# w3 and w_out chunks converted as one piece, ScalarE two units and VectorE one unit ahead, room for eight chunks, first loads on one queue

## The chip, the core and the metric

The kernel runs on one core of a Trainium2 chip. The core has five engines, each with an instruction queue that it works through in order: TensorE (PE in the profile; PEld is its weight load), VectorE (DVE), ScalarE (ACT), GpSimd (POOL) and SyncE (SP, which here only issues DMAs; ACT can issue DMAs too). They meet through semaphores. Matrix products go to PSUM, eight banks of 128 x 512 fp32, and are read from there by DVE or ACT.

The metric is the device time of one execution in microseconds. Three runs of the kernel before took 868.15, 868.35 and 868.7 us; the median is 868.35 us.

## The reference

```python
kv = np.einsum('bhsd,bhse->bhde', k, v)             # B, H, S, D = 8, 8, 576, 64
out = np.einsum('bhsd,bhde->bhse', q, kv)
rms = np.sqrt(np.mean(out * out, axis=-1, keepdims=True) + 1e-06)
x = (out / rms * g_norm)                            # then (B, H, S, D) -> (4608, 512)
a = x @ w1                                          # 512 x 1024
b = x @ w2
h = a * b @ w3                                      # 1024 x 1024
y = h @ w_out                                       # 1024 x 512
```

The weights arrive as 64-bit floats: `setup_inputs` scales fp32 arrays by a numpy scalar of 64 bits, which makes them double. Their conversion to fp32 is part of the kernel.

## The kernel before

**Stages.** The kernel first multiplies w3 by w_out once (the *fold*), so that each group of 512 tokens needs only x @ w1, x @ w2, the elementwise product, and one product with w3 @ w_out. Then it goes through nine groups: eight of 512 tokens, one for each batch, and a ninth made of the 64 tokens that each batch has left over. The products of a group are done by Winograd's scheme with seven products in place of eight (`winograd`, L436), on sums and differences of operand blocks that DVE prepares (`sum_w`, `combine_x` and the like).

**Conversion.** A 64-bit number lies in memory as two 32-bit words. `convert` (L127) makes fp32 of them with six instructions: ACT turns the low word into a small float (`low`, L135) and takes the absolute value of the high word read as fp32 (L136); DVE clamps that (L137), shifts its bits by three (L140), puts the sign bit into `low` (L143) and adds the two bit patterns (L147, a custom instruction, in the profile CUSTOM_DVE_ANT_0, in the lists of instructions ISA). The weights come in 20 *units* of 128 x 1024 numbers (1 MB as 64-bit floats), in the order of `todo` (L156): eight "c" units, each with the columns of the first half of w3 for one chunk and the chunk's 128 rows of w_out; four "b" units, each with the second half of w3 for two chunks; eight "w" units of w1 and w2. I number them 0 to 19: 0 to 7 are c, 8, 9, 11 and 13 are b, the rest w. Four raw buffers (`RAW = 4`) hold loaded units. `convert_next` (L194) converts the next unit and then has the load issued that takes its raw buffer (`load_next`, L164). A c unit is converted in two pieces of 512 columns, its w3 part and its w_out part (unit 0 in three); b and w units in one piece of 1024.

**The fold.** Two halves of eight chunks each. For a chunk, PE transposes four 128 x 128 blocks of w3 (`turn_w3`, L409, into a PSUM bank named `at`), ACT copies them to w3T (L416), and PE multiplies them with the chunk of w_out (`fold_chunk`, L420), adding over the chunks into four PSUM banks named `mm`. After the last chunk of a half, DVE and ACT copy two banks each to `w3o_sb` (L433, L431). The profile shows a step as eight matmuls of 128 x 512 (two for each product in the code) and four transposes. There are five `mm` banks and three `at` banks, and `w3_sb` holds two converted w3 pieces.

Half 0 has, for each chunk c: transposes of chunk c + 1, conversion of the unit after that, products of chunk c. Half 1 also carries the attention of the first batch, for four pairs of heads: `begin` (products of k and v, transposes of q, the loads of later heads), `middle` (product of q with kv, then the norm: square on ACT, sum on DVE, root on ACT, reciprocal and scaling on DVE) and `turn` (transposes of the result, copied with a scale to `xT` by ACT). After the fold, `sum_w(0)` and `combine_x(0)` prepare the operands of the first group on DVE, and the groups' loop begins; what is left of the conversion (units 16 to 19) stands in the first group.

**What sets the order.** PE's instructions are in the order of the code throughout. Those of DVE, ACT and SP are in the order of the code within the fold (`manual_schedule`, L613), and elsewhere a scheduler places them, which may also move instructions of later code into gaps that it sees in the fold.

**Names.** The lists of instructions and the profile leave out buffer numbers, and with them the digit of `w3_sb`: in the fold, `w_sb` is mostly the tile `w3_sb`; in conversions of w units it is the real `w_sb`.

Of the kernel before, what the change touches and what calls it, by code (L numbers as in the profile page):

```python
# [19 lines left out]
def kernel(  # L20
# [85 lines left out]
    def load_q_left(b):  # L106
# [5 lines left out]
        )  # L112


    w_sb = const.tile([P, KF, 2, NP, P], FP32, name="w_sb")
# [10 lines left out]

    def convert(dst, raw):  # L127
        if raw.dtype == FP32:
            nc.vector.tensor_copy(out=dst, in_=raw)
            return  # L130
        words = raw.bitcast(U32).rearrange("p (n w) -> p n w", w=2)
        lo, hi = words[:, :, 0], words[:, :, 1]
        low = conv_pool.tile([P, 1024], FP32, name="low", bufs=2)[:, 0:raw.shape[1]]
        dst_bits, low_bits = dst.bitcast(U32), low.bitcast(U32)
        nc.scalar.activation(low, lo, AF.Copy, scale=2.0 ** -51, bias=2.0)  # L135
        nc.scalar.activation(dst, hi.bitcast(FP32), AF.Abs)  # L136
        nc.vector.tensor_scalar(  # L137
            out=dst, in0=dst, scalar1=LEAST, scalar2=MOST, op0=ALU.max, op1=ALU.min
        )
# [3 lines left out]
        nc.vector.scalar_tensor_tensor(  # L143
            out=low_bits, in0=hi, scalar=0x80000000, in1=low_bits,
            op0=ALU.bitwise_and, op1=ALU.bitwise_or,
        )
        nc.vector.tensor_tensor(out=dst_bits, in0=dst_bits, in1=low_bits, op=ALU.add)  # L147
# [4 lines left out]

    NF = KF // 2
    RAW = 4
# [8 lines left out]

    def load_next(queue=nc.sync):  # L164
        if len(raws) == len(todo):
# [3 lines left out]

        def load(where, src, engine=nc.sync):  # L170
            engine.dma_start(out=raw[:, where].rearrange("p (c m) -> p c m", c=src.shape[1]), in_=src)

# [16 lines left out]
        raws.append(raw)  # L189

    converted = []
    w3_sb = {}

    def convert_next():  # L194
        n = len(converted)
        what, i = todo[n]
        if what == "w":
            convert(w_sb[:, i].rearrange("p w c f -> p (w c f)"), raws[n])
        elif what == "b":
            w3_sb["b", i] = fold.tile([P, 1024], FP32, name="w3_sb", bufs=2)  # L200
            convert(w3_sb["b", i], raws[n])
        else:
            t = w3_sb["c", i] = fold.tile([P, 1024], FP32, name="w3_sb", bufs=2)[:, 0:512]
            for cols in [slice(0, 512)] if i else [slice(0, 256), slice(256, 512)]:
                convert(t[:, cols], raws[n][:, cols])
            convert(wo_sb[:, i, :], raws[n][:, 512:1024])
        converted.append(n)
        load_next()
# [26 lines left out]
    def attention(b):  # L235
# [140 lines left out]
        if b == 0:  # L376
            return begin, middle, turn
        pieces = [
# [23 lines left out]

    ab = [const.tile([P, 4, N], FP32, name=f"ab{p}") for p in range(NF)]


    NH = KF // 2
    w3T = {}

    def turn_w3(half, c):  # L409
        t = w3_sb["b", c // 2] if half else w3_sb["c", c]  # L410
        t = t.rearrange("p (m f) -> p m f", m=NH)[:, :, (c % 2) * P * half:][:, :, 0:P]
        t_ps = bank(ps_at, "at").rearrange("p (m f) -> p m f", m=NH)
        for m in range(NH):
            nc.tensor.transpose(t_ps[:, m, :], t[:, m, :], ident)  # L414
        w3T[half, c] = fold.tile([P, NH, P], FP32, name="w3T", bufs=3)
        nc.scalar.copy(w3T[half, c], t_ps)  # L416

    sums_ps = {}

    def fold_chunk(half, c):  # L420
        if c == 0:
            sums_ps[half] = [bank(ps_mm, "mm") for m in range(NH)]
        for m in range(NH):
            nc.tensor.matmul(  # L424
                sums_ps[half][m], lhsT=w3T[half, c][:, m, :], rhs=wo_sb[:, c, :],
                start=(c == 0), stop=(c == KF - 1),
# [78 lines left out]
    xb, wa, aa, ob = {}, {}, {}, {}  # L505
    free = {}
    o_sbs = []

    def allocate():

        h = NP // 2
        for p in reversed(range(NF)):
            free["w", p] = late_pool.tile([P, 3, 2, h, P], FP32, name=f"ws{p}")
# [19 lines left out]
    def combine_x(T):  # L533
        xb[T] = {f"b{i + 1}{j + 1}": xT[T][:, i, j] for i in range(2) for j in range(2)}
        t = late_pool.tile([P, 3, NP // 2, N], FP32, name="xc")
        return combine(xb[T], parts(t))

# [41 lines left out]
    def project(T, between=lambda: None):  # L579
# [31 lines left out]
    fold = fold_cm.__enter__()  # L611
    wo_sb = fold.tile([P, KF, DM], FP32, name="wo_sb")
    in_order = tc.manual_schedule(  # L613
        engines={mybir.EngineType.DVE, mybir.EngineType.Activation, mybir.EngineType.SP}
    )
    with in_order:
        for _ in range(RAW):
            load_next(nc.scalar)
        g_src = g_norm.rearrange("(d o) -> d o", o=1)
        for e in range(2):  # L620
            nc.scalar.dma_start(out=g_col[e * D:(e + 1) * D, :], in_=g_src)
        nc.scalar.activation(const.tile([P, 1], FP32, name="warm"), eps_col, AF.Sqrt)


        keep_warm(14)
        convert_next()
        turn_w3(0, 0)
        convert_next()
        for c in range(KF):
            if c + 1 < KF:  # L630
                turn_w3(0, c + 1)
            else:
                turn_w3(1, 0)
            convert_next()
# [9 lines left out]
        begin, middle, turn = attention(0)  # L644
        AT = {1: 0, 3: 1, 4: 2, 5: 3}
        for c in range(KF):
            if c + 1 < KF:
                turn_w3(1, c + 1)
            if c in AT:
                begin(AT[c])  # L650
            if c < 6:
                convert_next()
            fold_chunk(1, c)
            if c in AT:
                middle(AT[c])
            if c - 1 in AT:
                turn(AT[c - 1])
    fold_cm.__exit__(None, None, None)
    late_pool = ctx.enter_context(tc.tile_pool(name="late", bufs=1, reuse_waits="tile"))
    allocate()  # L660
    run(sum_w(0), combine_x(0))

    for T in range(NG):
# [5 lines left out]
        for p in range(NF):  # L669
            gates(T, p, between if T or p else lambda: None)  # L670
            if T == 0:
                if p + 1 < NF:
                    run(sum_w(p + 1))
                for _ in range(2):
                    if len(converted) < len(todo):
                        convert_next()
                if p + 1 == NF:
# [39 lines left out]
```

## Time and profile before

| | |
|---|---|
| median of three runs | 868.35 us |
| the profiled execution | 869.37 us |
| its span, first to last instruction | 867.6 us |
| PE busy in the span | 830.0 us (96%) |
| DVE busy | 386.8 us (45%) |
| ACT busy | 267.5 us (31%) |
| granted PE clock, mean | 0.985 |
| DMA | 59.45 MB, mean 69 GB/s |

The shares are means over stages that differ. The page's row of 40 slices shows that DVE and ACT are busy mostly in the first six slices (130 us), that DMA moves 205 to 270 GB/s in the first five and little later, and that the granted clock falls below 0.9 only in the first, third and fifth slices. So the profile is read by stages: a table of windows first, then who waited for whom in the first stages, then single instructions in order of time. A row of such a list has the start in us, the length, engine and line, operation, output and input with their sizes, the number of instructions merged into the row, and in brackets how long the engine had been idle and what ended that.

### The profile page before, as it was taken

How to read it: one execution, taken by the hardware profiler on the slowest of the kernel's cores; microseconds unless marked ns; L12 is line 12 of the kernel's file. 1: busy time of each engine (PE TensorE's matmuls, PEld its weight loads, DVE VectorE, ACT ScalarE, POOL GpSimd, SP SyncE). 2: the span in 40 equal slices, each digit the busy share in tenths (PEclk: the TensorE clock that was granted, in tenths of full speed). 3: DMA queues.
4: the chain of work that ended last, by engine and by line, in shares of the span. 5: the costliest groups of instructions: out<-in, count | busy, mean ns of one | idle time of the engine just before them, and what ended most of it. 6: DMA issues, size and time to landing. Idle time of an engine off the chain costs nothing.

```text
span 867.6 us, 11176 instructions
## 1 busy us (share of the span) xinstructions
PE 830.0 (96%) x4556; PEld 699.8 (81%) x4556; DVE 386.8 (45%) x798; ACT 267.5 (31%) x521; POOL 0.7 (0%) x6
## 2 busy tenths in 40 slices
PE   4878689999999999999999999999999999999997
PEld 3334458888888888888888888888888888888886
DVE  5876699541543254324433353335234612432330
ACT  4554553422331234123312331233133312211210
POOL 0000000000000000000000000000000000000000
PEclk7999899999999999999999999999999999999999
DMA  7596622112220321022103110311030000001002
GB/s 255 205 270 220 210 64 86 52 35 84 64 60 0 97 73 50 1 85 73 49 0 119 54 49 1 108 51 49 6 117 1 1 15 34 1 1 49 1 0 50
DMA packets 57891, 59.45 MB, mean 69 GB/s; under 512 B 15344, under 2 KB 52208, under 8 KB 57840
## 3 DMA queue, kind: packets, MB, share of 16 engines
q1 hardware_dynamic: 57104, 56.63, 21.0%
q10 hardware_dynamic: 736, 2.10, 0.6%
q8 instruction: 36, 0.59, 0.3%
q14 instruction: 15, 0.12, 0.1%
HBM read 49.28 MB, written 9.44 MB: 68 GB/s over the span
## 4 chain that ended last, share of the span: by engine, by line
PE 88%; DVE 6%; ACT 4%; issue 1%; DMA 1%; ACTq 0%; SPq 0%; DVEq 0%
PE mm L443 75%; PE at L248 3%; PE at L315 3%; PE at L270 2%; DVE low L143 2%; DVE w_sb L147 2%; PE mm L424 2%; PE at L345 1%; ACT low L135 1%; ACT w_sb L136 1%; DVE w_sb L137 1%; DMA raw<-in_moe_w_dram 1%; PE at L414 1%; DVE w_sb L140 1%; PE at L332 1%
## 5 line engine op out<-in xcount | busy, mean ns | idle before, releaser
L443 PE MATMUL mm<-xT,w_sb 128*128 128x256 f32 x768 | 176.2, 379 | 0.0
L443 PEld LDWEIGHTS mm<-xT,w_sb 128*128 128x128 f32 x768 | 145.9, 190 | 20.3 <-issue 0.5
L443 PE MATMUL mm<-xc,ws 128*128 128x256 f32 x576 | 130.3, 379 | 0.0
L443 PEld LDWEIGHTS mm<-xc,ws 128*128 128x128 f32 x576 | 109.4, 190 | 15.2 <-DVE xc L485 0.4
L456 ACT COPY u<-mm 128x512 f32<-128x512 f32 x90 | 52.7, 585 | 207.6 <-PE mm L443 195.0
L443 PE MATMUL mm<-w3o_sb,ab 128*128 128x256 f32 x432 | 96.2, 379 | 0.0
L456 ACT COPY p<-mm 128x512 f32<-128x512 f32 x90 | 52.7, 585 | 140.7 <-PE mm L443 140.7
L443 PEld LDWEIGHTS mm<-w3o_sb,ab 128*128 128x128 f32 x432 | 82.1, 190 | 11.2
L443 PE MATMUL mm<-xc,w_sb 128*128 128x256 f32 x288 | 68.1, 379 | 0.0
L290 DVE TENSOR_REDUCE inv<-sq 128x8 f32<-128x512 f32 (+1 forms) x40 | 25.1, 628 | 90.1 <-ACT sq L288 90.1
L443 PE MATMUL mm<-raw 128*128 128x256 f32 x288 | 63.6, 379 | 0.0
L424 PE MATMUL mm<-wo_sb,w3T 128*128 128x512 f32 x128 | 63.4, 642 | 0.0
L569 DVE TENSOR_TENSOR c<-mm,u 128x512 f32<-128x512 f32 x36 | 24.5, 682 | 82.2 <-PE mm L443 82.2
L443 PE MATMUL mm<-xT,ws 128*128 128x256 f32 x256 | 60.8, 380 | 0.0
L443 PEld LDWEIGHTS mm<-raw 128*128 128x128 f32 x288 | 54.7, 190 | 7.4
L443 PEld LDWEIGHTS mm<-xc,w_sb 128*128 128x128 f32 x288 | 52.9, 190 | 6.2
L443 PEld LDWEIGHTS mm<-xT,ws 128*128 128x128 f32 x256 | 46.5, 190 | 5.4
L570 DVE TENSOR_TENSOR ab<-c 128x256 f32<-128x256 f32 x108 | 45.7, 423 | 2.9
L424 PEld LDWEIGHTS mm<-wo_sb,w3T 128*128 128x128 f32 x128 | 25.3, 209 | 26.7 <-issue 26.5
L598 DVE TENSOR_TENSOR raw<-mm,u 128x512 f32<-128x512 f32 x9 | 6.2, 693 | 85.7 <-issue 72.5
L569 DVE TENSOR_TENSOR c<-p,u 128x512 f32<-128x512 f32 x36 | 24.9, 692 | 35.1 <-ACT u L456 35.1
L262 DVE COPY kv_bd<-at 64x64 f32<-64x64 f32 x64 | 13.9, 217 | 54.5 <-PE at L248 53.9
(83 smaller groups left out, 865.3 us busy)
## 6 DMA issues: line engine op xcount, KB each, us to landing
raw<-in_moe_w_dram SPq DMA_DIRECT2D x23, 512.0 KB, 4.4
k_sb<-in_k_dram SPq DMA_DIRECT2D x32, 256.0 KB, 2.8
v_sb<-in_v_dram SPq DMA_DIRECT2D x32, 256.0 KB, 3.2
q_sb<-in_q_dram SPq DMA_DIRECT2D x32, 256.0 KB, 3.9
out_dram<-raw SPq DMA_DIRECT2D x16, 512.0 KB, 2.6
raw<-in_moe_w_dram SPq DMA_DIRECT2D x4, 1024.0 KB, 6.1
raw<-in_moe_w_out_dram ACTq DMA_DIRECT2D x4, 512.0 KB, 7.1
raw<-in_moe_w_out_dram SPq DMA_DIRECT2D x4, 512.0 KB, 4.5
```

The costliest lines, as they stand in the source:

```text
L143: nc.vector.scalar_tensor_tensor(out=low_bits, in0=hi, scalar=0x80000000, in1=low_bits, op0=ALU.bitwise_and, op1=ALU.bitwise_or,)
L147: nc.vector.tensor_tensor(out=dst_bits, in0=dst_bits, in1=low_bits, op=ALU.add)
L248: nc.tensor.matmul(kv_ps[e * D:(e + 1) * D, :], lhsT=k_sb[:, e, cols] if j < J else kl_sb[:, 2 * r + e, :], rhs=v_sb[:, e, cols] if j < J ...
L262: nc.vector.tensor_copy(out=dst, in_=src)
L270: nc.tensor.transpose(qt_ps[:, e, i, :], q_sb[:, e, i * P:(i + 1) * P], ident)
L290: nc.vector.tensor_reduce(out=inv, in_=sq[:, cols].rearrange("p (h d) -> p h d", d=D), axis=AX.X, op=ALU.add,)
L315: nc.tensor.matmul(o_ps[:, n * P:(n + 1) * P], lhsT=qT[r][:, e, i, :], rhs=bd[:, 2 * r + e, :], start=True, stop=True,)
L424: nc.tensor.matmul(sums_ps[half][m], lhsT=w3T[half, c][:, m, :], rhs=wo_sb[:, c, :], start=(c == 0), stop=(c == KF - 1),)
L443: nc.tensor.matmul(ps[:, u, :], lhsT=lhsT(a_name, u, c), rhs=rhs(b_name, c),  start=(u == 0 and c == 0 and to is None), stop=(c == chunks ...
L456: nc.scalar.copy(t, ps)
L569: nc.vector.tensor_add(c, one, two)
L570: nc.vector.tensor_mul(dst, c[:, 0, :], c[:, 1, :])
```

## The change

- A c unit is converted as one piece of 1024 columns (unit 0 still in three), straight into a tile `chunks` with room for all eight chunks of w3 and w_out side by side; b units are converted into the w3 part of the same tile. `low` and `w3T` lie in the tiles `ab` (numbered `ab_73` to `ab_76` in the lists), which the groups need only later.
- `convert_next` becomes `begin_next` (ACT's two instructions) and `end_next` (DVE's four, the sign step now first, then the load of the next unit). In half 0, ACT begins unit c + 2 and DVE ends unit c + 1 while PE is on chunk c.
- The transposes of the next chunk stand ahead of the last of a chunk's four products. In half 1 the order of attention's parts is changed: reciprocal and scaling of the norm stand a step later than sum and root. `sum_w(0)` and `combine_x(0)` move into the fold's last two chunks. `ws0` and `xc` get memory of their own.
- All raw loads are issued by SP, in the order of use; b units in two loads of 512 KB. On ACT the table load and `warm` stand ahead of g_col's loads.

The core of the diff:

```diff
+    ab = [const.tile([P, 4, N], FP32, name=f"ab{p}") for p in range(NF)]
-    def convert(dst, raw):
+    def conversion(n, dst, raw, cols=slice(0, 1024)):
...
-        low = conv_pool.tile([P, 1024], FP32, name="low", bufs=2)[:, 0:raw.shape[1]]
+        low = ab[NF - 2 + n % 2].rearrange("p i t -> p (i t)")[:, cols]
...
         nc.scalar.activation(low, lo, AF.Copy, scale=2.0 ** -51, bias=2.0)
         nc.scalar.activation(dst, hi.bitcast(FP32), AF.Abs)
+        yield
+        nc.vector.scalar_tensor_tensor(
+            out=low_bits, in0=hi, scalar=0x80000000, in1=low_bits,
+            op0=ALU.bitwise_and, op1=ALU.bitwise_or,
+        )
         nc.vector.tensor_scalar(
             out=dst, in0=dst, scalar1=LEAST, scalar2=MOST, op0=ALU.max, op1=ALU.min
         )
...
-            src = w3[DF // 2:DF, 2 * i * P:2 * (i + 1) * P].rearrange("(m p) f -> p m f", p=P)
-            load(slice(0, 1024), src)
+            for h in range(2):
+                src = w3[DF // 2:DF, (2 * i + h) * P:(2 * i + h + 1) * P]
+                load(slice(h * 512, (h + 1) * 512), src.rearrange("(m p) f -> p m f", p=P))
...
-            load(slice(512, 1024), src, queue)
+            load(slice(512, 1024), src)
...
+        dst = chunks[:, i].rearrange("p w f -> p (w f)")
+        cuts = [0, 1024] if i else [0, 256, 512, 1024]
+        return [conversion(n, dst, raws[n], slice(a, b)) for a, b in zip(cuts, cuts[1:])]
...
+    def begin_next():
+        if len(begun) < len(todo):
+            begun.append(conversions(len(begun)))
+            for c in begun[-1]:
+                next(c)
+
+    def end_next():
+        for c in begun[len(converted)]:
+            all_of(c)
+        converted.append(len(converted))
         load_next()
...
         for c in range(KF):
-            if c + 1 < KF:
-                turn_w3(0, c + 1)
+            if c == 0:
+                end_next()
+                begin_next()
             else:
-                turn_w3(1, 0)
-            convert_next()
+                begin_next()
+                end_next()
...
-            fold_chunk(0, c)
+            fold_chunk(0, c, range(NH - 1))
+            turn_w3(*((0, c + 1) if c + 1 < KF else (1, 0)))
+            fold_chunk(0, c, [NH - 1])
...
         for c in range(KF):
+            if c in AT:
+                begin(AT[c])
+            if c - 1 in AT:
+                all_of(norms[c - 1])
+            if c < KF - 2:
+                begin_next()
+                end_next()
+            elif c == KF - 2:
+                run(sum_w(0))
+            else:
+                run(combine_x(0))
+                end_next()
+            fold_chunk(1, c, range(NH - 1))
             if c + 1 < KF:
                 turn_w3(1, c + 1)
+            fold_chunk(1, c, [NH - 1])
             if c in AT:
-                begin(AT[c])
-            if c < 6:
-                convert_next()
-            fold_chunk(1, c)
-            if c in AT:
-                middle(AT[c])
+                norms[c] = product(AT[c])
+                next(norms[c])
+                next(norms[c])
             if c - 1 in AT:
                 turn(AT[c - 1])
...
-    run(sum_w(0), combine_x(0))
```

What stands in the queues shows it. First the start of ACT's queue, before, with the semaphores that a row waits for (DMAHW1 and DMAHW2 are those of the first two loads of unit 0):

```order
L171 DMA raw<-in_moe_w_out_dram 128x512 x4
L621 DMA g_col<-in_g_norm_dram 64x1 [waits DMAHW1_49]
L621 DMA g_col<-in_g_norm_dram 64x1 [waits DMAHW2_49]
L622 ACT_TABLE_LOAD
L622 ACTIVATE warm<-eps_col 128x1 [waits DVE_49]
L135 ACTIVATE low<-raw 128x256
L136 ACTIVATE w_sb<-raw 128x256
```

And now:

```order
L640 ACT_TABLE_LOAD
L640 ACTIVATE warm<-eps_col 128x1 [waits DVE_49]
L643 DMA g_col<-in_g_norm_dram 64x1 x2
L148 ACTIVATE ab_75<-raw 128x256 [waits DMAHW0_49]
L149 ACTIVATE chunks<-raw 128x256
```

The four loads of w_out have left the queue, and the table load and g_col's loads no longer stand behind a wait for a load.

Second, ACT in half 0: from one copy of w3T to the next but one, before.

```order
L416 COPY w3T<-at 128x512
L135 ACTIVATE low<-raw 128x512
L136 ACTIVATE w_sb<-raw 128x512
L135 ACTIVATE low<-raw 128x512
L136 ACTIVATE wo_sb<-raw 128x512
L416 COPY w3T<-at 128x512
```

And now, the unit's ACT part and the copies of w3T (into `ab_73`, `ab_74`), from the copy for the first chunk on:

```order
L437 COPY ab_73<-at 128x512
L148 ACTIVATE ab_76<-raw 128x1024
L149 ACTIVATE chunks<-raw 128x1024
L148 ACTIVATE ab_75<-raw 128x1024
L149 ACTIVATE chunks<-raw 128x1024
L437 COPY ab_73<-at 128x512
L148 ACTIVATE ab_76<-raw 128x1024
L149 ACTIVATE chunks<-raw 128x1024
L437 COPY ab_74<-at 128x512
```

A unit takes two instructions in place of four, and two units are begun behind the first copy, so that from there on each copy has ACT's part of one unit more ahead of it than DVE and PE need next.

Third, DVE at the end of half 1, around the copies to `w3o_sb` that free the PSUM banks of the fold. Before (`ws_775` and `xc` are the sums of the first group):

```order
L147 ISA w_sb<-w_sb,low 128x2048
L137 TENSOR_SCALAR w_sb<-w_sb 128x1024
L433 COPY w3o_sb<-mm 128x512
L140 TENSOR_SCALAR w_sb<-w_sb 128x1024
L143 SCALAR_TENSOR_TENSOR low<-raw,low 128x1024
L433 COPY w3o_sb<-mm 128x512
L495 TENSOR_TENSOR ws_775<-w_sb 128x512
L485 TENSOR_TENSOR xc<-xT 128x512
L496 TENSOR_TENSOR ws_775<-ws_775,w_sb 128x512
```

And now (the rows of L151 to L161 are steps of units 15 and 18):

```order
L506 TENSOR_TENSOR xc<-xT 128x512
L151 SCALAR_TENSOR_TENSOR ab_75<-raw,ab_75 128x1024
L506 TENSOR_TENSOR xc<-xT,xc 128x512
L506 TENSOR_TENSOR xT<-xT 128x512
L506 TENSOR_TENSOR xc<-xT,xc 128x512
L151 SCALAR_TENSOR_TENSOR ab_76<-raw,ab_76 128x1024
L155 TENSOR_SCALAR w_sb<-w_sb 128x1024 x2
L158 TENSOR_SCALAR w_sb<-w_sb 128x1024 x2
L161 ISA w_sb<-w_sb,ab_76 128x2048
L454 COPY w3o_sb<-mm 128x512 x2
L590 TENSOR_TENSOR c<-mm,u 128x512
```

The sums of the first group, which stood behind the copies, now stand ahead of them, and so do the first steps of unit 18 and the whole of unit 15.

More of the change, by code (lines that the diff above doesn't have):

```diff
@@ L125 @@
     )
-    def convert(dst, raw):
+    def conversion(n, dst, raw, cols=slice(0, 1024)):
+        dst, raw = (t if len(t.shape) == 3 else t[:, cols] for t in (dst, raw))
         if raw.dtype == FP32:
+            yield
             nc.vector.tensor_copy(out=dst, in_=raw)
@@ L168, in load_next, with load @@
         raw = raw_tile()
-        def load(where, src, engine=nc.sync):
-            engine.dma_start(out=raw[:, where].rearrange("p (c m) -> p c m", c=src.shape[1]), in_=src)
+        def load(where, src):
+            nc.sync.dma_start(out=raw[:, where].rearrange("p (c m) -> p c m", c=src.shape[1]), in_=src)
         if what == "w":
@@ L187, in load_next, with conversions @@
             src = w_out[i * P:(i + 1) * P, :].rearrange("p (c f) -> p c f", c=1)
-            load(slice(512, 1024), src, queue)
+            load(slice(512, 1024), src)
         raws.append(raw)
     converted = []
-    w3_sb = {}
-    def convert_next():
-        n = len(converted)
+    def conversions(n):
         what, i = todo[n]
         if what == "w":
[L198 to L207, printed above, removed]
+            return [conversion(n, w_sb[:, i].rearrange("p w c f -> p (w c f)"), raws[n])]
+        if what == "b":
+            return [conversion(n, chunks[:, 2 * i:2 * i + 2, 0, :], raws[n])]
+        dst = chunks[:, i].rearrange("p w f -> p (w f)")
+        cuts = [0, 1024] if i else [0, 256, 512, 1024]
+        return [conversion(n, dst, raws[n], slice(a, b)) for a, b in zip(cuts, cuts[1:])]
+    begun = []
+    def begin_next():
[7 more added lines that the diff above has]
+        converted.append(len(converted))
         load_next()
@@ L376, in attention @@
         if b == 0:
[L377 removed]
+            return begin, product, turn
         pieces = [
@@ L611 @@
     fold = fold_cm.__enter__()
-    wo_sb = fold.tile([P, KF, DM], FP32, name="wo_sb")
-    in_order = tc.manual_schedule(
+    chunks = fold.tile([P, KF, 2, DM], FP32, name="chunks")
+    with tc.manual_schedule(
         engines={mybir.EngineType.DVE, mybir.EngineType.Activation, mybir.EngineType.SP}
-    )
-    with in_order:
+    ):
         for _ in range(RAW):
-            load_next(nc.scalar)
+            load_next()
+        nc.scalar.activation(const.tile([P, 1], FP32, name="warm"), eps_col, AF.Sqrt)
         g_src = g_norm.rearrange("(d o) -> d o", o=1)
```

55 lines of the change are left out of this document (30 added, 25 removed).

## The prediction

> **What bounds the kernel now.** First the span cut into its stages, then who TensorE (PE) waits for in the first 121 us, then the instructions of one step. The stages are loading and first conversion, half 0 of the fold, half 1 of the fold with the first attention, and everything after it. Columns of the first rows: window, its length, busy time of PE, PEld, DVE, ACT, POOL, granted clock, DMA share, GB/s.
>
> ```profile
> 0.00:20.00 20.00, 8.87 (x38) 7.37 (x39) 10.60 (x23) 7.54 (x15) 0.70 (x6) 0.74 0.75 262
> 20.00:62.36 42.36, 34.92 (x96) 15.70 (x95) 31.75 (x57) 22.59 (x37) 0.00 (x0) 0.92 0.77 228
> 62.36:120.29 57.93, 44.66 (x234) 25.52 (x233) 41.55 (x60) 34.73 (x53) 0.00 (x0) 0.94 0.64 201
> 120.29:867.60 747.31, 741.57 (x4193) 651.21 (x4191) 302.92 (x662) 202.63 (x418) 0.00 (x0) 1.00 0.14 44
> ```
>
> From 120.29 us on PE is busy for 741.57 of 747.31 us. The change leaves PE's work there as it is, so it can win or lose little there, and I cost that stage at nothing (within 2 us). Everything is decided in the first 120 us.
>
> ```profile
> PE at L414 <- DVE w_sb L147: 17.2, 9, 5.1
> PE at L345 <- DVE xn L300: 5.5, 2, 3.1
> PE at L270 <- ACT w3T L416: 5.3, 1, 5.3
> ```
>
> There PE waits above all for the last step of a conversion (17.2 us in 9 waits), then for attention's norm, then for a copy of w3T. One step of half 0, in order of time (start, length, engine, instruction):
>
> ```profile
> 29.28 0.63 PE L414 MATMUL at<-ident,w_sb 128*128 128x128 f32 x4 [0.71 <-DVE w_sb L147]
> 30.00 0.58 ACT L416 COPY w3T<-at 128x512 f32<-128x512 f32 x1 [1.96 <-PE at L414]
> 30.48 0.69 ACT L135 ACTIVATE low<-raw 128x512 f32<-128x512 uint32 x1
> 33.29 0.69 DVE L147 CUSTOM_DVE_ANT_0 w_sb<-w_sb,low 128x1024 uint16<-128x1024 uint16 x1
> 34.13 0.63 PE L414 MATMUL at<-ident,w_sb 128*128 128x128 f32 x4 [0.78 <-DVE w_sb L147]
> ```
>
> This is a closed loop: transposes, copy of w3T, ACT's part of the next conversion behind that copy, DVE's part, next transposes: 34.13 - 29.28 = 4.85 us. No engine is full; each waits for the one before it.
>
> **The change, part by part.** *Start.* ACT issues its loads, then g_col's two, and only then loads its table:
>
> ```profile
> 5.77 2.65 ACTq L621 DMA_DIRECT2D g_col<-in_g_norm_dram  x2
> 8.45 1.28 ACT L622 ACT_TABLE_LOAD   x1 [8.45 <-DMA raw<-in_moe_w_dram]
> 9.86 0.41 ACT L135 ACTIVATE low<-raw 128x256 f32<-128x256 uint32 x1
> 24.97 3.60 PE L424 MATMUL mm<-wo_sb,w3T 128*128 128x512 f32 x8
> 0.00:4.00 4.00, 2.65 (x12) 2.65 (x13) 1.88 (x3) 0.00 (x0) 0.70 (x6) 1.00 0.43 132
> 4.00:6.00 2.00, 2.00 (x12) 2.00 (x10) 0.00 (x0) 0.00 (x0) 0.00 (x0) 1.00 0.96 353
> 6.00:8.00 2.00, 0.99 (x8) 0.80 (x7) 0.00 (x0) 0.00 (x0) 0.00 (x0) 1.00 1.03 406
> ```
>
> In the change the table load stands first and g_col's issues wait for no load. All loads stand on SP in the order of use, and I take it that they also move in that order. By 4 us 0.53 MB have moved (132 GB/s x 4 us), which is the w3 part of unit 0; its w_out part (1.05 MB in all) comes by 5.5 us, unit 1 (2.1 MB) by about 8.2 us. With half a microsecond allowed until an engine sees it, ACT begins at about 4.5 instead of 9.86 us. That SP issues nine loads one after another costs about 4 us for the last, which belongs to unit 3, not needed before 15 us. Unit 0 is then converted by about 9 us, unit 1 by 13.5 us. Its transposes, the last product of the chunk before and the w3T copy put the second chunk's products at about **15 us instead of 24.97**: 10 us won. Loads that share the engines evenly, as now, would give 17; the best is 13.5.
>
> *Half 0.* Conversion is begun two units ahead, so the loop is cut; each engine now has its own rate. Rows for the 1024-wide unit, which half 1 has already, and for PE when it doesn't wait:
>
> ```profile
> 59.70 0.69 DVE L137 TENSOR_SCALAR w_sb<-w_sb 128x1024 f32<-128x1024 f32 x1 [3.52 <-ACT w_sb L136]
> 63.43 0.68 DVE L433 COPY w3o_sb<-mm 128x512 f32<-128x512 f32 x1
> 50.16 1.16 ACT L135 ACTIVATE low<-raw 128x1024 f32<-128x1024 uint32 x1
> 51.20 1.13 ACT L136 ACTIVATE w_sb<-raw 128x1024 f32<-128x1024 f32 x1
> 62.36 3.60 PE L424 MATMUL mm<-wo_sb,w3T 128*128 128x512 f32 x8
> 65.80 0.60 PE L414 MATMUL at<-ident,w_sb 128*128 128x128 f32 x4
> 66.33 0.69 PE L248 MATMUL at<-v_sb,k_sb 128*64 128x64 f32 x16
> 67.20 0.66 PE L270 MATMUL at<-ident,q_sb 128*128 128x128 f32 x4
> 67.70 3.60 PE L424 MATMUL mm<-wo_sb,w3T 128*128 128x512 f32 x8
> 71.13 1.05 PE L315 MATMUL at<-kv_bd,qT 128*128 128x128 f32 x8
> 72.02 0.60 PE L414 MATMUL at<-ident,w_sb 128*128 128x128 f32 x4
> ```
>
> DVE needs 63.43 - 59.70 = 3.73 us for a unit; its new order keeps the four instructions. ACT needs 2 x 1.04 us and 0.58 for the copy, 2.7 us. PE needs 65.80 - 62.36 = 3.44 us for a chunk's products and 66.33 - 65.80 = 0.53 for transposes: 3.97. PE is the slowest, barely. The w3T copy (0.58) lies beside the chunk's last product (a quarter of 3.44, 0.86). Loads of 1.05 MB every 4 us are 260 GB/s, below the 406 above. Between the second chunk's products and the first of half 1 lie seven steps: before 62.36 - 24.97 = 37.4, then 7 x 3.97 = 27.8 us: **9.6 us won**, half 1 starting at about 42.8. If the loop stays closed, the old pace is the other end: nothing won.
>
> *Half 1.* PE alone: eight chunks at 3.97, without the last transposes, 31.2; four times attention: kv 0.87 (66.33 to 67.20), q transposes 0.50, product 0.89 (71.13 to 72.02), xn transposes again 0.53: 2.79, in all 11.2. So the fold would end at 42.8 + 42.4 = 85 us, some 86 with short waits. The second product of the first group, though, needs a PSUM bank that a w3o copy on DVE frees, and in the changed order those copies stand behind nearly all of DVE's early work: sixteen whole conversions after unit 0, pieces of two more, attention, sum_w(0) and combine_x(0). Durations for these:
>
> ```profile
> 76.42 0.68 DVE L290 TENSOR_REDUCE inv<-sq 128x8 f32<-128x512 f32 x1
> 77.46 0.20 DVE L299 RECIPROCAL inv<-inv 128x8 f32<-128x8 f32 x1 [0.37 <-ACT inv L297]
> 77.77 0.69 DVE L300 TENSOR_TENSOR xn<-at,inv 128x512 f32<-128x512 f32 x1
> 69.05 0.47 DVE L262 COPY kv_bd<-at 64x64 f32<-64x64 f32 x2
> 120.86 0.68 DVE L495 TENSOR_TENSOR ws<-w_sb 128x512 f32<-128x512 f32 x1
> 121.46 0.68 DVE L485 TENSOR_TENSOR xc<-xT 128x512 f32<-128x512 f32 x1
> 122.20 3.72 PE L443 MATMUL mm<-xc,ws 128*128 128x256 f32 x16
> 93.14 1.11 PE L270 MATMUL at<-ident,q_sb 128*128 128x128 f32 x4 [5.34 <-ACT w3T L416]
> 94.04 5.70 PE L424 MATMUL mm<-wo_sb,w3T 128*128 128x512 f32 x8
> raw<-in_moe_w_dram SPq DMA_DIRECT2D x23, 512.0 KB, 4.4
> ```
>
> Units 1 to 16: 16 x 3.73 = 59.7. Unit 0 in three pieces: estimated 4.9 (one unit and two more starts). Pieces of two later units (one sign step, two clamps, two shifts: a little over one unit): 4.0. Attention: 4 x (0.47 + 0.68 + 0.2 + 0.69) = 8.2. Eight sums at 0.60 (121.46 - 120.86): 4.9. The two w3o copies of half 0: 1.3. Together 83.0 us, from about 4.5 us on: **87.5 us with no idle time on DVE**. Laying the queues beside each other, I find 5 to 6 us of it (kv copies waiting for PE, reductions waiting for ACT's squares). So the copies run at about 93, and the second product starts at **93.5 instead of 122.20**, PE having waited some 5 us. The bounds are 88 (PE is the limit) and 100.
>
> *A cold clock.* After a wait of 5.34 us the q transposes took 1.11 instead of 0.66 and the products 5.70 instead of 3.60. I charge 2.1 us for PE's wait before the second product (bounds 0 and 2.5). The Trainium skill, "TensorE: Matmul & The Clock Gate", Part 1 (The HAM clock gate), says that after an idle window of about 3.4 us the array runs at half its clock until it has been busy for about 3.4 us. By that rule the charge would be 1.7 us and the sum 0.4 us better; the rows here show more, so they are kept.
>
> *Costed at nothing.* Abs, clamp, shift and add on a strided destination: same elements, beside PE. The b units in two 512 KB loads instead of one: needed some 8 us after issue, against 4.4 to landing. ws0 and xc in memory of their own, low and w3T in ab: no new instruction; ab's first late use follows the last conversion on DVE itself. combine_x of later groups earlier on DVE: PE is busy there. If that cover went, each group could lose about 0.7 us per sum.
>
> *The sum.* 122.20 - 93.5 - 2.1 = 26.6 us. The profiled execution took 869.37 us (span 867.6 and 1.77 around it), so 842.8. The median shown is 868.35, 1.02 lower, so **842** for the runs. What is late next is DVE's queue, not PE.
>
> **The rivals.** *DVE keeps up.* If its waits don't add up, or the copies come early enough, PE goes straight on from 86 us and the second product starts at 88, with no cold clock: 34 us won, 834. For it: PE's own sum. Against it: DVE's sum without any idle time is already 87.5. *Loads are late.* In the changed ACT order an Abs of units 16, 17 and 19 stands ahead of a w3T or a PSUM copy, and ACT takes its queue in order. If unit 16 or 17 isn't there, ACT waits up to one landing (4.4 us), PE and DVE behind it, and the clock falls (1.7 to 2.1): 6 us lost, 848. It decides when SP, whose queue also holds attention's loads waiting for PE, issues that load under 5 us before its use. I find some 5 us of room for 17, and none for 19. *The pace of half 0 stays.* The change would then not do what it says: 4.85 instead of 3.97 in seven steps, 6.2 us lost, 848. Against it: nothing in the rows closes the loop any more. *Slower.* If one queue in order sustained only about 150 GB/s, each unit would take 7 us; fifteen steps from 15 us on and attention's 11.2 put the first group at 131 us, 9 later than 122.2: 877. It decides where a step takes 6.4 us (15 + 15 x 6.4 + 11.2 = 122.2), 165 GB/s; half 0 moves 228 now, all but the first loads from SP.
>
> **How the numbers follow.** DVE's queue, 842: 0.50 (alone it spans 838 to 846). DVE keeps up, 834: 0.15. Late loads, 848: 0.18. Old pace, 848: 0.12. Slower, 877: 0.03. Something that eats all of it: 0.02. From 833.5 to 851 no more than 2 in 10 is left out: part of the first rival, the last two, and late loads twice over. Faster by over 0.2% (1.7 us, about what a measurement of this kernel can tell from no change): 0.95; within: 0.02; slower: 0.03.
>
> **What would show it.** Right: table load near 1 us and ACT's first conversion before 5.5 us; steps of half 0 of 3.9 to 4.1 us, with PE waiting under 0.2 us in each; half 1's first products at 41 to 44 us; the first w_sb product of the first group near 86 to 89, the second near 93, and DVE without gaps of over a microsecond from 64 us on; a granted clock of 0.50 just after. Wrong: PE waiting for an ACT copy that stands behind a load; steps above 4.5 us; the second product right behind the first; any new wait of PE after 130 us.

## The result, and the profile after

| | before | after |
|---|---|---|
| median, 4 runs each | 868.53 us | 839.62 us (838.66 to 840.17) |
| profiled execution / span | 869.37 / 867.6 us | 840.17 / 838.4 us |
| PE busy in the span | 96% | 98% |
| ratio of times | | 0.9657 [0.9628, 0.9685] |

The change wins 28.9 us of the medians and 29.2 us of the spans. It was run a second time beside the last experiments (label after_again): 839.18 us, ratio 0.9633 [0.9608, 0.9658].

> The changed kernel itself once more, beside the next three on the same chip: 839.6 within 0.7, as before.

The windows of the changed kernel, cut at the row that holds the second chunk's products, at the row that holds half 1's first products, and at the first product of the first group; the columns are those of the prediction's first rows:

```profile
0.00:16.82 16.82, 10.39 (x42) 7.24 (x43) 11.03 (x20) 9.15 (x13) 0.70 (x6) 0.90 0.84 288
16.82:44.73 27.91, 27.91 (x87) 12.79 (x85) 26.09 (x30) 19.52 (x22) 0.00 (x0) 1.00 1.06 324
44.73:91.16 46.43, 44.54 (x240) 25.84 (x239) 39.09 (x57) 33.42 (x51) 0.00 (x0) 0.96 0.89 272
91.16:838.40 747.24, 741.31 (x4193) 651.29 (x4191) 308.31 (x666) 206.40 (x422) 0.00 (x0) 1.00 0.14 44
```

Two of these cuts are not quite those of before. The transposes of the next chunk now stand ahead of the last product of a chunk, so the rows at 16.82 and 44.73 us begin with that last product (two matmuls), and the next chunk's own products begin 0.9 us later, at 17.68 and 45.62. Cut there, the stages take 17.68, 27.94, 45.54 and 747.24 us; before, they took 24.97, 37.4, 57.93 and 747.31. So 7.3 us come from the start, 9.5 from half 0, 12.4 from half 1, and nothing from the rest: 29.2. In half 0 PE is now busy without a gap, and the page's row of the granted clock has no slice below 0.9 any more (before, the first and the fifth were).

PE's waits in the first 100 us of the changed kernel (total, times, longest):

```profile
PE mm L445 <- DVE chunks L161: 4.1, 1, 4.1
PE mm L254 <- POOL ident masks.py:199: 1.4, 1, 1.4
PE at L292 <- ACT xT L369: 1.2, 1, 1.2
PE at L432 <- DVE chunks L161: 0.9, 2, 0.5
PE at L270 <- ACT ab L437: 0.7, 1, 0.7
```

Of the 17.2 us for conversions 5.0 are left, all at the start; the 5.5 for attention's norm are gone. The 1.4 us for `ident` are there in both kernels. Two short waits for ACT are left in half 1. The start in order of time, with a window of it at the end (the last number is GB/s):

```profile
0.74 1.28 ACT L640 ACT_TABLE_LOAD   x1 [0.74 <-PEq L739]
3.57 0.43 ACT L148 ACTIVATE ab<-raw 128x256 f32<-128x256 uint32 x1 [1.34 <-DMA raw<-in_moe_w_dram]
8.46 0.66 ACT L148 ACTIVATE ab<-raw 128x512 f32<-128x512 uint32 x1 [2.68 <-DMA raw<-in_moe_w_out_dram]
11.31 1.12 ACT L148 ACTIVATE ab<-raw 128x1024 f32<-128x1024 uint32 x1 [1.16 <-DMA raw<-in_moe_w_out_dram]
16.82 3.68 PE L445 MATMUL mm<-chunks,ab 128*128 128x512 f32 x8
4.00:6.00 2.00, 2.00 (x18) 2.00 (x17) 1.88 (x6) 1.11 (x4) 0.00 (x0) 1.00 0.52 151
```

ACT begins at 3.57 us, but waits for w_out of unit 0 until 8.46 and for unit 1 until 11.31. From 4 to 6 us the loads move 151 GB/s, where they moved 353 before. Then half 1 where PE waits, and the place on which the prediction's sum rested, the first two products of the first group and the copies that free the fold's banks:

```profile
72.22 1.17 ACT L149 ACTIVATE w_sb<-raw 128x1024 f32<-128x1024 f32 x1 [0.56 <-DMA raw<-in_moe_w_dram]
73.29 0.57 ACT L437 COPY ab<-at 128x512 f32<-128x512 f32 x1
73.91 0.69 PE L270 MATMUL at<-v_sb,k_sb 128*64 128x64 f32 x16 [0.71 <-ACT ab L437]
76.03 1.06 PE L292 MATMUL at<-ident,q_sb 128*128 128x128 f32 x4 [1.18 <-ACT xT L369]
76.89 4.06 PE L445 MATMUL mm<-chunks,ab 128*128 128x512 f32 x6
89.65 0.59 ACT L452 COPY w3o_sb<-mm 128x512 f32<-128x512 f32 x1
91.16 1.89 PE L464 MATMUL mm<-xT,w_sb 128*128 128x256 f32 x8
91.36 0.59 ACT L452 COPY w3o_sb<-mm 128x512 f32<-128x512 f32 x1
92.89 3.62 PE L464 MATMUL mm<-xc,ws 128*128 128x256 f32 x16
97.76 1.28 DVE L454 COPY w3o_sb<-mm 128x512 f32<-128x512 f32 x2
```

The second product follows the first without a wait, almost 5 us before DVE's copies. So the bank that it takes is not one of DVE's; ACT's two copies have ended by 91.95 us.

### The profile page after: what moved, and what is told of

It reads as the page before. It is cut to its first block, busy times and chain, and to the rows that moved or that the text cites. A ratio compares the mean times of both kernels' runs of the same rounds, so it can differ in the third digit from the quotient of the medians.

```text
span 838.4 us, 11142 instructions
## 1 busy us (share of the span) xinstructions
PE 824.1 (98%) x4556; PEld 697.2 (83%) x4556; DVE 384.5 (46%) x770; ACT 268.5 (32%) x507; POOL 0.7 (0%) x6
## 4 chain that ended last, share of the span: by engine, by line
PE 95%; DMA 2%; DVE 1%; ACT 1%; issue 0%; SPq 0%; ACTq 0%; DVEq 0%
PE mm L464 78%; PE mm L445 5%; PE at L337 3%; PE at L270 3%; PE at L292 2%; PE at L367 2%; DMA raw<-in_moe_w_out_dram 1%; DMA raw<-in_moe_w_dram 1%; PE at L354 1%; PE at L432 1%; DVE ab L151 0%; SPq L184 0%; PE at L376 0%; PE at L302 0%; DVE chunks L158 0%
## 5 line engine op out<-in xcount | busy, mean ns | idle before, releaser
L445 PE MATMUL mm<-chunks,ab 128*128 128x512 f32 x128 | 62.6, 624 | 4.1 <-DVE chunks L161 4.1
L445 PEld LDWEIGHTS mm<-chunks,ab 128*128 128x128 f32 x128 | 23.1, 200 | 27.3 <-issue 21.9
```

What stands on the lines that cost most here:

```text
L445: nc.tensor.matmul(sums_ps[half][m], lhsT=w3T[half, c][:, m, :], rhs=chunks[:, c, 1, :], start=(c == 0), stop=(c == KF - 1),)
```

## The experiments

All edits are to the changed kernel unless said otherwise. Times are medians of 4 or 5 runs; the ratio is to the kernel before on the same chip. Where a kernel has the new order of the loop, "the row of the second chunk" is the row at 16.82 us above, and its time is compared with that row alone; the chunk's own products begin 0.9 us later in each. The intervals are 0.6% wide, so differences of 1 to 3 us between two kernels are read from the traces, beside the medians.

**The predicted wait, put there.** All four copies of half 1 on DVE.

```diff
-                if m % 2:
+                if m % 2 and half == 0:
                     nc.scalar.copy(dst, sums_ps[half][m])
```

> All four w3o copies of half 1 on DVE instead of two, so that the second product of the first group must wait for a copy on DVE: the wait that the prediction charged and that the changed kernel doesn't have. The copies run there at about 97.8 us. Theory: the prediction's mechanism was sound but the bank that is taken is one that ACT frees; with it forced onto DVE the second product starts at 98.5 instead of 92.9, PE's clock falls behind the wait, and the time rises by 5.6 plus 1.5 to 2: 847. Rival: PE finds another way to keep busy or the gap is made up in the first group: under 842.

Measured: 846.61 us, 0.9714 [0.9684, 0.9743]. The first two products in its timeline, then a window behind the wait (the seventh number is the granted clock):

```profile
89.16 1.89 PE L464 MATMUL mm<-xT,w_sb 128*128 128x256 f32 x8
96.65 5.89 PE L464 MATMUL mm<-xc,ws 128*128 128x256 f32 x16 [5.60 <-DVE w3o_sb L454]
97.00:101.00 4.00, 4.00 (x10) 3.19 (x10) 4.00 (x7) 0.68 (x2) 0.00 (x0) 0.50 0.00 0
```

A wait of 5.60 us and 5.89 instead of 3.62 us for the matmuls behind it: 7.9 us, and 7.0 in the medians. The prediction had charged 5 and 2.1. So the mechanism and its price were right, and it is not in the changed kernel, because there ACT's copies free a bank in time. (The span grows by 6.0 us only, since this execution reaches the first group 2.0 us earlier, at 89.16.)

**The start, undone in two steps.** First all of it, then with the table load and `warm` left ahead of g_col's loads.

```diff
-            load_next()
+            load_next(nc.scalar)      # w_out of units 0 to 3 on ACT's queue
-        nc.scalar.activation(..., name="warm"), eps_col, AF.Sqrt)
         ...                           # g_col's two loads
+        nc.scalar.activation(..., name="warm"), eps_col, AF.Sqrt)
```

> The changed kernel with the start of before: the first four w_out loads on ACT's queue, g_col's loads ahead of the table load. If the gains of the three stages add up independently, as the trace says, the second chunk's products go back from 16.82 to about 25 us and the time rises by 8 us, to 848; half 0's seven steps stay at 28 us, half 1 at 46. Rival: the later stages, which also run ahead on loads, make up for a late start or lose more by it: under 845 or over 851.

> Splits the gain of the start: the first four w_out loads on ACT's queue as before, but the table load and warm still ahead of g_col's loads. If the order on ACT is what won (table load not behind a wait for a load), most of the 8 us stays: 839 to 841. If one queue in the order of use is what won, it goes: about 846. By the trace of the changed kernel, where w_out of unit 0 came only at 8.46 us from the one queue, two queues could even be better by 1 to 2 us, since SP issues about two loads a microsecond.

Measured: 842.45 us, 0.9664 [0.9636, 0.9692], and 840.86 us, 0.9651 [0.9623, 0.968]. The row of the second chunk starts at 20.93 and 18.84 us. From the first kernel, that row and the wait in half 1; from the second, g_col's issues and ACT's first conversion:

```profile
20.93 3.68 PE L445 MATMUL mm<-chunks,ab 128*128 128x512 f32 x8
79.56 0.66 PE L292 MATMUL at<-ident,q_sb 128*128 128x128 f32 x4 [1.18 <-ACT xT L369]
80.06 2.74 PE L445 MATMUL mm<-chunks,ab 128*128 128x512 f32 x6
```

```profile
5.68 2.64 ACTq L643 DMA_DIRECT2D g_col<-in_g_norm_dram  x2
8.36 0.43 ACT L148 ACTIVATE ab<-raw 128x256 f32<-128x256 uint32 x1 [3.78 <-DMA raw<-in_moe_w_dram]
```

The first expectation was off: the row comes at 20.93 and not at 25. So of the 7.3 us of this stage 4.1 belong to ACT's order and the loads; the other 3.2 belong to the rest of the change. The second's time lies in its first case (839 to 841), but by the trace only two of the 4.1 us come from the table load ahead of g_col's loads (20.93 to 18.84). The other two came with the single queue, and that edit does two things. The two w3 loads of unit 0 take 5.8 us from issue to landing with two queues (the median), 3.3 with one. And with w_out on ACT's queue g_col's issues wait for these two loads again, ahead of ACT's first conversion, which follows the second issue at once, at 8.36 us (its row names a load as what ended the wait, but the first of the two had landed at 5.7). What each of these costs was not measured apart.

In the total the start is worth 2.8 us, not 4.1, since with the late start half 1, from its row to the first group, takes 44.7 us instead of 46.4 (48.83 to 93.53): the same wait of 1.18 us is there, but the clock doesn't fall behind it.

**g_col's loads later.** Moved from ACT's start to the fourth step of half 0.

```diff
-        g_src = ...                   # and two loads on ACT's queue
         keep_warm(14)
...
+            if c == 3:
+                g_src = ...           # and two loads on ACT's queue
```

> The two small loads of g_col (64 pieces of 4 bytes each) moved from ACT's start to half 0. The changed kernel moves only 50 to 160 GB/s between 3.9 and 5.6 us, just when these loads are under way. If they hold the others up, w_out of unit 0 lands at about 7 instead of 8.46 us, the second chunk's products start 1 to 1.5 us earlier, and the time is 838.3. If the dip comes from the one queue of large loads itself, nothing moves: 839.6 within 0.5.

Measured: 839.47 us, 0.9631 [0.9603, 0.9659]; the row of the second chunk at 16.16. That is 0.66 earlier than in the first profile of the changed kernel, but its second profile (after_again) has it at 16.15 too. Nothing is shown to be won.

**No look-ahead in half 0**, with one piece, one queue and room for eight chunks kept.

```diff
         begin_next()
+        end_next()
         for c in range(KF):
-
-            if c == 0:
-                end_next()
-                begin_next()
-            else:
-                begin_next()
+            turn_w3(*((0, c + 1) if c + 1 < KF else (1, 0)))
+            begin_next()
+            if c + 1 < KF:
                 end_next()
...
-            fold_chunk(0, c, range(NH - 1))
-            turn_w3(*((0, c + 1) if c + 1 < KF else (1, 0)))
-            fold_chunk(0, c, [NH - 1])
+            fold_chunk(0, c, range(NH))
```

> The changed kernel with one piece, one queue and eight chunks of room, but in half 0 unit c + 2 is begun and ended behind the transposes of chunk c + 1, as before, and those transposes stand ahead of all four products. Theory: the loop of before is closed again, and longer with one piece: transposes and copy about 1.2 us, ACT's first instruction 1.1, DVE 3.8, a step of about 6.2 us against 3.97; over seven steps 15 us more, 854 or so. Rival: the one piece and the room for eight chunks are what won in half 0: steps under 4.85, under 846.

Measured: 858.76 us, 0.9854 [0.9823, 0.9884]. One step of it, from one row of transposes to the next:

```profile
48.15 0.63 PE L432 MATMUL at<-ident,chunks 128*128 128x128 f32 x4 [2.27 <-DVE chunks L161]
48.61 3.60 PE L445 MATMUL mm<-chunks,ab 128*128 128x512 f32 x8
54.49 0.63 PE L432 MATMUL at<-ident,chunks 128*128 128x128 f32 x4 [2.28 <-DVE chunks L161]
```

Steps of 6.34 us, 2.3 of them a wait for the conversion. The loop is there again. The look-ahead, with the place of the transposes that goes with it, is worth 19 us of the 29. The second chunk's own products come at 23.38 us instead of 17.68, a part that my 854 had left out, and half 0 takes 15 us more (43.0 instead of 27.9). Half 1 isn't hurt: it takes 44.0 us. The steps are longer than those of before with its two pieces (4.85 us); that the one piece does this was the expectation, and no run tests it alone.

**Two pieces for each unit, look-ahead kept.**

```diff
-        cuts = [0, 1024] if i else [0, 256, 512, 1024]
+        cuts = [0, 512, 1024] if i else [0, 256, 512, 1024]
```

> The changed kernel, but each c unit from the second on converted in two pieces of 512 columns, as before; the look-ahead stays. By the rows of the 512-wide piece DVE then needs 4.26 us for a unit instead of 3.73, more than PE's 3.97. Theory: half 0 becomes bound by DVE, its seven steps take 29.8 instead of 27.9 us, and with the first unit the time is about 842. Rival: the one piece matters more than that, because ACT pays for four starts too and the loop closes again: steps above 4.5 us, 844 or more. Or it matters not at all, since later waits absorb it: under 840.5.

Measured: 839.17 us, 0.9631 [0.9603, 0.9659]: no loss. The end of half 0:

```profile
39.95 3.93 PE L445 MATMUL mm<-chunks,ab 128*128 128x512 f32 x8
44.90 0.63 PE L432 MATMUL at<-ident,chunks 128*128 128x128 f32 x4 [1.02 <-DVE chunks L161]
45.36 1.02 PE L445 MATMUL mm<-chunks,ab 128*128 128x512 f32 x2
```

DVE is the slower engine there, 4.26 us for a unit, but it is a unit ahead, and eight units are over before that lead is used up: PE waits 1.02 us once, at the last step. The row of the second chunk comes at 16.06 us, against 16.82 and 16.15 in the two profiles of the changed kernel, so no gain is shown at the start; half 1 passes without the fall of the clock. As a part of its own, the one piece brings nothing that these runs can show.

**Half 1.** The norm in place in one kernel, the first sums issued behind the fold in another.

```diff
-            if c - 1 in AT:
-                all_of(norms[c - 1])
...
-                norms[c] = product(AT[c])
-                next(norms[c])
-                next(norms[c])
+                all_of(product(AT[c]))
```

```diff
-            elif c == KF - 2:
-                run(sum_w(0))
-            else:
-                run(combine_x(0))
+            elif c == KF - 1:
                 end_next()
...
     allocate()
+    run(sum_w(0), combine_x(0))
```

> Half 1 of the changed kernel with the norm's reciprocal and scaling again straight behind the root, instead of a step later. In the kernel before, PE waited 5.5 us in two waits for the scaled xn. Theory: DVE now waits for ACT's root four times, about a microsecond each, in a half where it is close to full, and half 1 grows from 46.4 to 48 us: 841. Rival: the waits of before came from DVE being late with conversions, not from the norm's place: no change, 839.6 within 0.5.

> sum_w(0) and combine_x(0) issued behind the fold, as before, instead of in its last two chunks (they keep memory of their own, and the scheduler may still place some of them into the fold; in its order the four sums of w go ahead, the last two of xc stand behind unit 15). Theory: the second product needs only the first sums, PE does not wait, 839.6 within 1. Rival: moving the sums is what brought the second product from 122 to 93 us: then it waits for DVE again, 843 or more.

Measured: 841.66 us, 0.966 [0.9627, 0.9693], and 841.96 us, 0.9664 [0.9635, 0.9693]. PE's wait in each, and for the second kernel also ACT's:

```profile
76.84 0.66 PE L292 MATMUL at<-ident,q_sb 128*128 128x128 f32 x4 [2.31 <-ACT xT L369]
```

```profile
77.04 1.12 PE L292 MATMUL at<-ident,q_sb 128*128 128x128 f32 x4 [3.17 <-ACT xT L369]
77.95 5.12 PE L445 MATMUL mm<-chunks,ab 128*128 128x512 f32 x6
76.11 0.30 ACT L319 ACTIVATE inv<-inv,eps_col 128x8 f32<-128x8 f32 x1 [2.01 <-DVE inv L312]
```

The split norm saves 1.1 us of a wait, and it is one for ACT's xT copy; the medians differ by 2.0 us, and the intervals can't tell. The place of the sums acts in a way that neither theory had: issued behind the fold, the four sums of w are placed by the scheduler into the middle of half 1 (from 66.38 us on), and DVE's later work with them, its reduction among it, stands later; ACT's root waits 2.01 us for it, the xT copy stands behind the root, and PE waits 3.17 us. Writing them into the last two chunks kept them out of the way.

These two parts, undone, cost about 2 us each of the 12.4 us that half 1 won. In half 1 of the kernel before, PE waited five times, 13.2 us together, and now twice, 1.9 us. Of the 5.5 us for xn the norm in place brings back only 0.8. The longest wait of before, 5.3 us for a w3T copy, comes back in no run, but the traces tell how it came about. ACT's root waits for DVE's reduction, and what stands behind the root waits too; before and now (total, times, longest):

```profile
ACT inv L297 <- DVE inv L290: 8.3, 3, 4.0
ACT inv L319 <- DVE inv L312: 3.4, 4, 1.1
```

In the kernel before, the w3T copy at 92.52 us stood right behind such a root, which had waited 3.44 us. Which part of the change shortened these waits was not undone by itself and stays open; it was not the look-ahead in half 0, since half 1 keeps its 44.0 us without that.

**Improvements.** ACT's part of the units in the first group in code order; then, added to it, attention's `turn` ahead of the next `product`, g_col's loads later and unit 1 in two pieces; then a hold on the loads of units 2 and 3.

```diff
+                with tc.manual_schedule(engines={mybir.EngineType.Activation}):
                     for _ in range(2):              # no_hoist
...
-            if c in AT:
-                norms[c] = product(AT[c])
-                ...
             if c - 1 in AT:
                 turn(AT[c - 1])
+            if c in AT:                             # combined
+                norms[c] = product(AT[c])
+                ...
...
+        if len(raws) == 2:                          # combined_gate
+            nc.gpsimd.tensor_copy(raw.bitcast(FP32)[:, 0:1], raws[0].bitcast(FP32)[:, 2047:2048])
```

> ACT's two instructions for units 16 to 19 kept in the order of the code, so that no Abs of theirs stands ahead of half 1's w3T copies. In the changed kernel one such Abs ran from 72.22 us after a wait of 0.56 for its load; PE then waited 0.71 for the w3T copy behind it and 1.18 for a copy of xT, and the clock fell for 4 us. Theory: these are the small version of the rival of late loads; without them half 1 shrinks by 1 to 3 us, 837.5. Rival: the Abs only fill idle time of ACT (with the late start PE waited the same 1.18 us without any wait for a load), and what isn't done in the fold must be done in the first group: 839.6 to 842.

> The former, and three more small ones: attention's transposes and xT copy ahead of the next product and its root (ACT's xT copy no longer behind a root that waits 0.75 us for DVE), g_col's loads later, unit 1 in two pieces. Theory: PE alone sets the first 100 us, so each microsecond of its waits that goes is won: 0.7 plus 0.7 at the start, 1.2 at the xT copy, and the former's: 835.5. Rival: DVE's queue is next. Its copies to w3o ended at 99.0 us in the changed kernel, less than a microsecond before the product with a12, which needs another bank; if that is a bound, the gain ends there: not below 838.5.

> The former, with the loads of units 2 and 3 held until w_out of unit 0 has landed (a one-column copy on POOL into unit 2's buffer waits for it), so that they don't share the DMA engines with units 0 and 1. If sharing is what made w_out of unit 0 land at 8.46 us and unit 1 at 11.31 in the changed kernel, the second chunk's products come another 1 to 2 us earlier, 834.5; if the loads are limited by their own issue and latency, nothing is won, and unit 2 is late instead: 836 or more.

Measured beside 839.18 us for the changed kernel itself: 838.4 us (0.9628 [0.9602, 0.9653]), 838.29 (0.9615 [0.9589, 0.9641]) and 838.06 (0.9618 [0.9592, 0.9643]). The medians fall by 0.8 to 1.1 us; the intervals overlap. Without the early Abs, the wait of 0.71 us for w3T is gone, that for xT is 1.06, and one of 0.7 for a scaled xn is new; with `turn` first, the one for xT is gone too. From combined, the start, a new wait, and the place where DVE's copies stand:

```profile
10.95 5.46 PE L445 MATMUL mm<-chunks,ab 128*128 128x512 f32 x6 [3.15 <-DVE chunks L161]
10.00:14.00 4.00, 3.05 (x4) 1.51 (x5) 3.86 (x9) 2.37 (x5) 0.00 (x0) 0.54 1.05 380
14.00:18.00 4.00, 4.00 (x10) 1.72 (x8) 3.90 (x6) 2.48 (x4) 0.00 (x0) 0.61 1.07 372
85.00 0.63 PE L367 MATMUL at<-ident,xn 128*128 128x128 f32 x4 [0.99 <-DVE xn L322]
95.80 3.62 PE L464 MATMUL mm<-xT,w_sb 128*128 128x256 f32 x16
96.70 1.28 DVE L454 COPY w3o_sb<-mm 128x512 f32<-128x512 f32 x2
99.54 1.99 PE L464 MATMUL mm<-xc,w_sb 128*128 128x256 f32 x8
```

The first group starts at 88.89 us instead of 91.16, but PE now waits 0.99 us for a scaled xn from DVE, and the sixteen matmuls from 95.80 on take 3.74 us to the next row instead of 3.45: the second eight of them, the product with a12, start about when the copies end. DVE is next in two places, as the rival said. Its floor of 838.5 us doesn't hold: of the five runs of combined, two took 836.5 and 836.97 us at a mean clock of 0.998 and 0.997, the others 838.3 to 838.5 at 0.994. In the profiled one the clock is low for most of 8 us at the start. The gate brought nothing: w_out of unit 0 landed at 7.82 us (7.78 in the second profile of the changed kernel), so it isn't the later loads that hold it up.

## Why the prediction was right, step by step

**Start: the second chunk's products predicted at 15 us, 17.68 measured (17.01 in the second profile).** The table load (0.74 us) came as foreseen, and ACT's first conversion earlier (3.57 instead of 4.5). The loads landed in the order of use, but the step that failed is their rate: for 4 to 6 us 353 GB/s were put in, and 151 moved (228 in the second profile). So w_out of unit 0 was put at 5.5 us and came at 8.46, unit 1 at 8.2 and came at 11.31. And the 10 us were put down to the loads and the table load; by the two runs above these make 4.1 of the 7.3 us, and the rest of the change 3.2.

**Half 0: 27.8 predicted, 27.94 measured.** PE's own rate, 3.96 to 4.01 us a step. The cause holds: without the look-ahead the step is 6.3 us. That DVE must need no more than PE's 3.97 us for a unit was taken as a condition, and isn't one over eight steps, as two_pieces shows.

**Half 1: 42.4 predicted for PE alone and 86 us for its end; 45.54 and 91.16 measured.** Its first products came at 45.62 us, outside the 41 to 44 that the prediction gave as a sign of being right. The forecast left out 0.71 + 1.18 us of waits for ACT, and 1.7 us of slow matmuls behind them (q transposes 1.06 instead of 0.66, six products 4.06 instead of 2.74); 2.7 us of the lateness came from the start. The rival of late loads was there in small: an Abs ahead of a w3T copy, waiting 0.56 us for its load.

**Second product: 93.5 predicted with a wait of 5 us for a copy on DVE; 92.89 measured, with none.** This is the step that was wrong. I had taken it that the bank is one of those that DVE copies; it is freed by ACT. The second product right behind the first, which the prediction named as a sign of being wrong, is what came, and so the outcome of the rival "DVE keeps up". But DVE did not keep up: its copies ran at 97.76, later even than the 93 forecast. Its work was summed about right (80.5 us busy from 4.5 us to the copies, 83.0 forecast); its idle time was not (12.8 us instead of 5 to 6). w3o_on_dve shows the forecast's wait with its price.

**The sum: 26.6 predicted, 29.2 measured.** The forecast's second product at 93.5 with 2.1 us for the clock behind it stands against 92.89 with none: 2.7 us, the whole difference between the 842.8 us forecast for the profiled execution and its 840.17. That the sum is so near is luck: two errors went against each other. PE reached the first group 5 us later than forecast, and the wait of 5 us and the cold clock there did not come.

**Costed at nothing:** the strided destinations, the split b loads, the tiles in `ab` and the sums of later groups. The last stage took 747.24 against 747.31 us, as forecast, and clamp and shift on `chunks` take 0.69 us each, as before. **The old pace** of half 0 and **the slower case** did not come: loads moved 324 GB/s in half 0.

## What to carry to other kernels

A closed loop over three engines, each far from full, is worth more than any single duration in it: here beginning a unit earlier on one engine, with the transposes placed later, won 19 of 29 us, while the shape of the pieces didn't matter over eight steps once the lead was there. Before a wait for a buffer is charged, find out which engine frees the buffer that is taken; the same code with the copies on the other engine differed by 7 us. And undo each part by itself: the gains of a start are partly given back at the next place where an engine is short, and parts seen apart don't add up.

## What was unexpected in the hardware

The clock of TensorE falls behind the same wait in some executions and not in others. The wait of 1.18 us for xT in half 1, with one of 0.71 or less ahead of it, was followed by six products in 4.06 us in the first profile of the changed kernel and in 4.44 us in the second and in g_col_late, and in 2.74 us in start_undone and w3o_on_dve; a wait of 2.31 us in norm_in_place was also followed by 2.74. The Trainium skill, "TensorE: Matmul & The Clock Gate", Part 1 (The HAM clock gate), says that the activity window is free-running and that the number of cold matmuls therefore varies from run to run. The runs here agree with that: the five of combined, one kernel, had mean clocks from 0.994 to 0.998. But no wait ahead of these falls was as long as the 3.4 us that this section of the Trainium skill gives for an idle window. One such fall costs about 1.7 us here (4.44 instead of 2.74), so differences of that size between kernels of this kind are to be read with the granted clock beside them.
